# A gated attention and gelu MLP on one Trainium2 core: the gelu's square taken from ScalarE to GpSimd, and the copies of the turned maxima from ScalarE to VectorE

## The chip, the core and the metric

The kernel runs on one NeuronCore of one Trainium2 chip. The metric is the device time of one execution in microseconds (us). The kernel before takes 812.53 us, the median of three runs (812.45, 812.53 and 814.32). In the profile the engines have short names: PE is TensorE (its weight loads stand apart as PEld), DVE is VectorE, ACT is ScalarE, POOL is GpSimd, and SP is SyncE, which only issues transfers here.

## What is computed

```python
x = A_x                                    # 1 x 2048 x 512, float32
g = sigmoid((x * gate_w).sum(-1, keepdims=True))
# a: attention, 32 heads of 16, a query sees itself and the 255 keys before it
scores = q k^T * 16 ** -0.5, masked outside the window
a = (softmax(scores) v) @ wo               # wqkv is 512 x 1536, wo 512 x 512
# b: dense layers with a gelu (tanh form)
b = gelu(x @ w1 + b1) @ w2 + b2            # w1 is 512 x 1792, w2 1792 x 512
out = g * a + (1 - g) * b
```

## The kernel before

The dense products keep float32 accuracy by splitting each factor into a rounded high part and a low rest. The helper `mm3` (lines 100 to 103) then issues three matmuls, high by high, high by low and low by high. That is why each dense group in the profile appears three times, at L101, L102 and L103.

The program has three stretches. First come q, k and v for four blocks of 512 rows, until about 150 us. Then the attention and the MLP run interleaved until about 770 us. The output projection and the mix with the gate come last.

The attention goes in 128 units: 8 groups of 4 heads by 16 blocks of 128 keys. For each of a unit's 4 heads TensorE first computes scores `sm` with queries on the partitions (L389). VectorE adds the mask and takes each query's maximum in one custom instruction (L394; its output `jm` is scrap, the maximum goes to `M` by a short read of the accumulator). This runs six units ahead of the rest. Every two units the eight maxima per query are negated and laid out in `nm` by two small VectorE instructions (L405, L406). A matmul with the identity turns them so that queries lie along the free dimension (L413, PSUM tile `mp`). Two copies, one for each unit, put 16 rows of 256 numbers into rows 96 to 111 of `qs`, scaled by a column of `odd` that is 0 or 1 for each row (L418). The later score matmul `st` (L433) has these rows among its inputs and so subtracts the maximum. ScalarE takes the exponential into `pt` (L445), GpSimd zeroes what lies outside the window (L437, L440), and the products with v accumulate in `pv` (L465).

The MLP goes in eight passes, each over one half of the 1792 hidden columns and one block of 512 rows. A pass first makes 7 hidden tiles `u` (12 matmuls each), and then 4 output tiles `y` (21 matmuls each). I call these the u-phase and the y-phase of a pass. In the u-phase each tile goes through the gelu:

- `x1` = u + b1, ScalarE (L556)
- `sq` = (u + b1) squared, ScalarE, from PSUM (L559)
- `sq` = (sq + 22.36) * x1, VectorE (L562)
- `sq` = tanh of that, ScalarE (L565)
- `x1` = (sq + 1) * x1, VectorE (L568), then the high part `h[:, 0]`, VectorE (L571), then the low part `h[:, 1]`, GpSimd (L574)

Some buffers are scarce: `x1` and `sq` have two each, the PSUM tag `sm` (shared by `sm` and `mp`) three, `st` two, and `d` (for `u` and `y`) two.

The order on every engine is fixed while the program is built. A clock of planned nanoseconds moves with the matmuls that are written (`tick`), and `after(ns, fn)` writes a step into its engine's queue when that clock has passed. So a step's delay is only a place in the queue. On the chip an engine runs its queue strictly in order, and a step whose inputs are late holds everything behind it. The six delays of the gelu's steps after `x1` stand in the tuple `GELU`. Weights for later passes are loaded and split between the gelus: the high part on ScalarE (L156), the low part on GpSimd (L160).

Of the kernel before, what the change touches and what calls it, by code (L numbers as in the profile page):

```python
# [12 lines left out]
AF = mybir.ActivationFunctionType  # L13
ALU = mybir.AluOpType
# [18 lines left out]
def gated_mix(ctx: ExitStack, tc: tile.TileContext, x, wqkv, wo, w1, b1, w2, b2, gate_w, out):  # L33
    nc = tc.nc
# [10 lines left out]
    def f32(ap):  # L45
        return ap.bitcast(F32)
# [23 lines left out]
    b1c = cp.tile([128, NF], F32, name="b1c")  # L70
# [15 lines left out]
    odd = cp.tile([128, 2], F32, name="odd")  # L86
# [21 lines left out]
    def after(ns, fn, *args):  # L108
        now[1] += 1
        heapq.heappush(todo, (now[0] + ns, now[1], fn, args))  # L110
# [7 lines left out]
    def tick(ns):  # L118
        now[0] += ns
        while todo and todo[0][0] <= now[0]:  # L120
            step_todo()

    def need(*keys):
        for key in keys:
            while key not in done:
                step_todo()
# [51 lines left out]
    qs = cp.tile([128, 2, S], F32R, name="qs")  # L178
# [230 lines left out]
    def att_turn(g_, rb):  # L409

        need(("nm", g_, rb))
        p = ps.tile([112, 128], F32, tag="sm", bufs=3, name=f"mp{g_}_{rb}")
        nc.tensor.matmul(p, nms[rb % 2], identr, start=True, stop=True)  # L413

        def put():
            for b in range(RB):
                cols = slice((rb * RB + b) * 128, (rb * RB + b + 1) * 128)
                nc.scalar.activation(qs[96:112, :, cols], p[96:112].unsqueeze(1).broadcast_to([16, 2, 128]),  # L418
                    AF.Copy, scale=odd[96:112, b:b + 1])
            done.add(("rows", g_, rb))  # L420
        tick(67)
        after(100, put)
# [129 lines left out]
    def gelu(p, f, h):  # L552

        x1 = sb.tile([128, T], F32, tag="x1", bufs=2, name=f"x1{h.name}")
        sq = sb.tile([128, T], F32, tag="sq", bufs=2, name=f"sq{h.name}")
        nc.scalar.activation(x1, p, AF.Identity, bias=b1c[:, f:f + 1])  # L556

        def f1():
            nc.scalar.activation(sq, p, AF.Square, bias=b1c[:, f:f + 1])  # L559

        def f2():
            nc.vector.scalar_tensor_tensor(sq, sq, GC, x1, op0=ALU.add, op1=ALU.mult)  # L562

        def f3():
            nc.scalar.activation(sq, sq, AF.Tanh, scale=GS)  # L565

        def f4():
            nc.vector.scalar_tensor_tensor(x1, sq, 1.0, x1, op0=ALU.add, op1=ALU.mult)  # L568

        def f5():  # L570
            nc.vector.tensor_copy(h[:, 0], x1)  # L571

        def f6():
            nc.gpsimd.tensor_sub(h[:, 1], x1, f32(h[:, 0]))  # L574
            done.add(h.name)
        for ns, fn in zip(GELU, (f1, f2, f3, f4, f5, f6)):
            after(ns, fn)
# [168 lines left out]
LEAD = 6  # L746
START = 117e3
NORM = 6000
GELU = (700, 1500, 2300, 3300, 4200, 5000)
XAT = 3  # L750
ORDER = 'mspf'
XOR = 1
# [26 lines left out]
```

## Time and profile before

| profiled execution before | |
|---|---|
| its own time | 813.36 us |
| span in the trace | 811.4 us |
| PE busy | 788.5 us, 97% |
| DVE busy | 513.7 us, 63% |
| ACT busy | 483.4 us, 60% |
| POOL busy | 338.7 us, 42% |

The span runs from the first to the last instruction in the trace; the time of the execution holds 2.0 us more around it. A busy time is the union of an engine's instructions. In a table by windows each engine has its busy time and, in brackets, how many instructions; after them stand the clock that TensorE was granted, the DMA engines' share and GB/s. In a list of groups a row gives line, engine, operation, output and input, shape and count, then total busy us and mean ns of one, and then how long the engine sat idle just before such instructions and who ended that. A row of waits reads: who waited, for whom, us in total, how often, the longest.

### The profile page before, as it was taken

To read this page: it belongs to the slowest core of one execution; us is meant where nothing else is said; L and a number is where in the kernel's file an instruction comes from. 1 tells how busy PE (TensorE), PEld (TensorE's weight loads), DVE (VectorE), ACT (ScalarE), POOL (GpSimd) and SP (SyncE) were. 2 spreads that over 40 slices of the span, in tenths; PEclk is the share of its full clock that TensorE was granted. 3 is DMA by queue.
4 is the path that set the end of the run, shared out by engine and by line. 5 is a ranking of instruction groups with operands and counts; after the bars stand their busy time and mean duration, and the time that the engine had idled before them with its cause. 6 is when DMAs were issued, how large, how long until landed. Compare 5 with 4: busy or idle time off the path is not lost.

```text
span 811.4 us, 14841 instructions
## 1 busy us (share of the span) xinstructions
PE 788.5 (97%) x4694; PEld 616.6 (76%) x4694; DVE 513.7 (63%) x1517; ACT 483.4 (60%) x993; POOL 338.7 (42%) x611
## 2 busy tenths in 40 slices
PE   8999999999999999999999999999999999999998
PEld 6788888867877777688767867877777778777767
DVE  5433332887478758856885688568757865784353
ACT  4434423587568557755875677567656764876631
POOL 3200002396336425542784386336524552574100
PEclk9999999999999999999999999999999999999999
DMA  8985856536542734443234555542664363335873
GB/s 260 387 308 195 304 174 211 195 89 215 164 137 66 227 116 119 122 156 104 86 101 132 171 156 173 152 143 86 192 179 129 99 202 113 97 118 186 249 260 117
DMA packets 94925, 135.72 MB, mean 167 GB/s; under 512 B 32256, under 2 KB 43776, under 8 KB 94848
## 3 DMA queue, kind: packets, MB, share of 16 engines
q1 hardware_dynamic: 94848, 134.79, 52.3%
q8 instruction: 37, 0.61, 0.3%
q14 instruction: 40, 0.33, 0.1%
HBM read 79.70 MB, written 55.05 MB: 166 GB/s over the span
## 4 chain that ended last, share of the span: by engine, by line
PE 78%; DVE 8%; ACT 7%; DMA 2%; issue 2%; SPq 1%; POOL 1%; POOLq 0%; DVEq 0%; ACTq 0%
PE st L433 9%; PE pv L465 9%; PE sm L389 8%; PE y L101 6%; PE y L103 6%; PE y L102 6%; PE u L101 4%; PE u L102 4%; PE u L103 4%; PE qk L101 3%; PE qk L103 3%; PE qk L102 3%; DVE jm L394 2%; ACT pt L445 2%; PE v L103 2%
## 5 line engine op out<-in xcount | busy, mean ns | idle before, releaser
L394 DVE CUSTOM_DVE_ANT_0 jm<-sm,mask 128x384 bf16<-128x384 f32 (+2 forms) x512 | 270.6, 528 | 150.1 <-PE sm L389 128.7
L445 ACT ACTIVATE pt<-st 128x384 f32<-128x384 f32 (+2 forms) x512 | 231.0, 471 | 120.6 <-PE st L433 102.9
L437 POOL TENSOR_SCALAR_AFFINE_SELECT pt<-pt 128x256 f32<-128x256 f32 x256 | 122.3, 478 | 248.8 <-ACT pt L445 248.2
L433 PE MATMUL st<-qs,ks 128*128 128x384 f32 (+2 forms) x512 | 172.1, 338 | 8.1 <-ACT pt L445 7.1
L389 PE MATMUL sm<-ks,qs 96*128 96x384 f32 (+2 forms) x512 | 169.6, 332 | 1.8 <-DVE M L394 0.8
L433 PEld LDWEIGHTS st<-qs,ks 128*128 128x128 f32 x512 | 97.0, 190 | 37.1 <-ACT pt L445 19.4
L389 PEld LDWEIGHTS sm<-ks,qs 96*128 96x128 f32 x512 | 96.2, 188 | 26.0 <-DVE M L394 5.2
L440 POOL TENSOR_SCALAR_AFFINE_SELECT pt<-pt 128x256 f32<-128x256 f32 x224 | 101.9, 455 | 0.0
L465 PE MATMUL pv<-pt,vbuf 128*32 128x384 f32 (+2 forms) x1408 | 91.6, 389 | 0.1
L101 PE MATMUL y<-w,h 128*128 128x512 f32 x224 | 89.4, 399 | 0.0
L103 PE MATMUL y<-w,h 128*128 128x512 f32 x224 | 87.7, 391 | 1.3 <-POOL h L574 1.3
L102 PE MATMUL y<-w,h 128*128 128x512 f32 x224 | 87.7, 391 | 0.0
L574 POOL TENSOR_TENSOR h<-x1h,h 128x512 fp32r<-128x512 f32 x56 | 72.5, 1294 | 35.6 <-DVE h L571 35.2
L101 PE MATMUL u<-mx,w 128*128 128x512 f32 x196 | 79.3, 404 | 0.0
L102 PE MATMUL u<-mx,w 128*128 128x512 f32 x196 | 76.7, 391 | 0.0
L103 PE MATMUL u<-mx,w 128*128 128x512 f32 x196 | 76.6, 391 | 0.0
L418 ACT ACTIVATE qs<-mp,odd 16x256 fp32r<-16x256 f32 x128 | 53.0, 460 | 38.9 <-PE mp L413 37.9
L465 PEld LDWEIGHTS pv<-pt,vbuf 128*32 128x32 f32 x1408 | 38.5, 109 | 37.2 <-issue 24.2
L562 DVE SCALAR_TENSOR_TENSOR sqh<-sqh,x1h 128x512 f32<-128x512 f32 x56 | 51.6, 921 | 13.2 <-ACT sqh L559 13.2
L565 ACT ACTIVATE sqh<-sqh 128x512 f32<-128x512 f32 x56 | 35.5, 634 | 36.8 <-DVE sqh L562 36.2
L160 POOL TENSOR_TENSOR w<-raw_w,w 128x512 fp32r<-128x512 f32 x28 | 38.4, 1370 | 40.3 <-ACT w L156 40.2
L256 DVE TENSOR_TENSOR qke<-qk,qke 128x512 fp32r<-128x512 f32 x32 | 22.1, 691 | 51.3 <-ACT qke L253 49.6
(122 smaller groups left out, 1247.7 us busy)
## 6 DMA issues: line engine op xcount, KB each, us to landing
mx<-XT SPq DMA_DIRECT2D x24, 512.0 KB
SQ<-qke SPq DMA_DIRECT2D x16, 512.0 KB
SK<-qke SPq DMA_DIRECT2D x16, 512.0 KB
qs<-SQ SPq DMA_DIRECT2D x64, 128.0 KB
ND<-nd SPq DMA_DIRECT2D x32, 256.0 KB
ks<-SK SPq DMA_DIRECT2D x60, 128.0 KB
raw_w<-in_B_w_dram SPq DMA_DIRECT2D x28, 256.0 KB
SV<-vx SPq DMA_DIRECT2D x16, 272.0 KB
```

The costliest lines, as they stand in the source:

```text
L101: nc.tensor.matmul(p, lh, rh, start=first, stop=False)
L102: nc.tensor.matmul(p, lh, rl, start=False, stop=False)
L103: nc.tensor.matmul(p, ll, rh, start=False, stop=last)
L389: nc.tensor.matmul(p[:, :w], qs[0:96, pr, b * 128:(b + 1) * 128], ks[0:96, pr, s, k0:k0 + w], start=True, stop=True)
L394: nc.vector.tensor_tensor_reduce(junk[:, :w], p[:, :w], mask[:, 384 - w:384], 1.0, -3e38, ALU.add, ALU.max, M[:, b % RB, i:i + 1])
L418: nc.scalar.activation(qs[96:112, :, cols], p[96:112].unsqueeze(1).broadcast_to([16, 2, 128]), AF.Copy, scale=odd[96:112, b:b + 1])
L433: nc.tensor.matmul(p[:, :w], ks[:, pr, s, kb * 128:(kb + 1) * 128], qs[:, pr, kb * 128:kb * 128 + w], start=True, stop=True)
L437: nc.gpsimd.affine_select(out=pt[:, :, 0:128], in_=pt[:, :, 0:128], pattern=[[0, 2], [1, 128]], compare_op=ALU.is_ge, fill=0.0, base=0, ch ...
L440: nc.gpsimd.affine_select(out=pt[:, :, 256:384], in_=pt[:, :, 256:384], pattern=[[0, 2], [-1, 128]], compare_op=ALU.is_ge, fill=0.0, base= ...
L445: nc.scalar.activation(pt[:, s, :w], p[:, :w], AF.Exp, scale=SCALE)
L465: nc.tensor.matmul(pv[32 * i:32 * i + 32, q - c * T:e - c * T], vt[:, 68 * (kb % NB) + 17 * i:68 * (kb % NB) + 17 * i + 32], pts[g_, kb, i ...
L574: nc.gpsimd.tensor_sub(h[:, 1], x1, f32(h[:, 0]))
```

## The change

Two steps leave ScalarE, and the planned delays of the gelu change with them. The copies of the turned maxima become a `tensor_scalar` on VectorE, with the same input (PSUM, each row read twice), the same scale and the same place in the program. The square becomes a product of `x1` with itself on GpSimd; it reads `x1` from SBUF, since GpSimd is given no PSUM tile in this kernel. The first delay stays 700, the others grow by 700.

```diff
@@ att_turn
         def put():
             for b in range(RB):
                 cols = slice((rb * RB + b) * 128, (rb * RB + b + 1) * 128)
-                nc.scalar.activation(qs[96:112, :, cols], p[96:112].unsqueeze(1).broadcast_to([16, 2, 128]),
-                    AF.Copy, scale=odd[96:112, b:b + 1])
+                nc.vector.tensor_scalar(qs[96:112, :, cols], p[96:112].unsqueeze(1).broadcast_to([16, 2, 128]),
+                                        odd[96:112, b:b + 1], None, op0=ALU.mult)
@@ gelu
         def f1():
-            nc.scalar.activation(sq, p, AF.Square, bias=b1c[:, f:f + 1])
+            nc.gpsimd.tensor_mul(sq, x1, x1)
@@
-GELU = (700, 1500, 2300, 3300, 4200, 5000)
+GELU = (700, 2200, 3000, 4000, 4900, 5700)
```

TensorE's queue is the same in both kernels, instruction by instruction. On VectorE, here is a piece of the third u-phase in the kernel before. In a name like `sqh1_3` the numbers are the block of rows and the hidden tile; `jm2_10_3` is group 2, unit 10, head 3; longer numbers only count buffers.

```order
L406 SCALAR_TENSOR_TENSOR nm0_170<-M2_8_3688,nm0_170 128x8
L394 ISA jm2_10_0_3843,M2_10_3820<-sm2_10_0_3841,mask_140 128x384
L394 ISA M2_10_3820 128x1
L562 SCALAR_TENSOR_TENSOR sqh1_4_3829_3836<-sqh1_4_3829_3836,x1h1_4_3829_3835 128x512
L394 ISA jm2_10_3_3857,M2_10_3820<-sm2_10_3_3855,mask_140 128x384
L394 ISA M2_10_3820 128x1
L568 SCALAR_TENSOR_TENSOR x1h1_4_3829_3835<-sqh1_4_3829_3836,x1h1_4_3829_3835 128x512
L394 ISA jm2_10_2_3885,M2_10_3820<-sm2_10_2_3883,mask_140 128x384
```

And this is the same piece of VectorE's queue in the changed kernel.

```order
L406 SCALAR_TENSOR_TENSOR nm0_170<-M2_8_3687,nm0_170 128x8
L394 ISA jm2_10_0_3842,M2_10_3820<-sm2_10_0_3840,mask_140 128x384
L394 ISA M2_10_3820 128x1
L394 ISA jm2_10_3_3856,M2_10_3820<-sm2_10_3_3854,mask_140 128x384
L394 ISA M2_10_3820 128x1
L562 SCALAR_TENSOR_TENSOR sqh1_4_3828_3835<-sqh1_4_3828_3835,x1h1_4_3828_3834 128x512
L418 TENSOR_SCALAR qs_179<-mp2_4_3872,odd_164 16x2x128 x2
L394 ISA jm2_10_2_3884,M2_10_3820<-sm2_10_2_3882,mask_140 128x384
L568 SCALAR_TENSOR_TENSOR x1h1_4_3828_3834<-sqh1_4_3828_3835,x1h1_4_3828_3834 128x512
```

The gelu's first VectorE step stands one maximum later than before, and the two copies of the turned maxima stand between it and the next maximum.

On GpSimd, this is the same place before: the selects (L437, L440) of units 3 and 4, and the low part of tile 3.

```order
L437 AFFINE_SELECT pt2_3_0_3774<-pt2_3_0_3774 128x2x128
L440 AFFINE_SELECT pt2_3_0_3774<-pt2_3_0_3774 128x2x128
L437 AFFINE_SELECT pt2_3_1_3798<-pt2_3_1_3798 128x2x128
L440 AFFINE_SELECT pt2_3_1_3798<-pt2_3_1_3798 128x2x128
L574 TENSOR_TENSOR h1_3_3758<-x1h1_3_3758_3764,h1_3_3758 128x512
L437 AFFINE_SELECT pt2_4_0_3824<-pt2_4_0_3824 128x2x128
```

And in the changed kernel:

```order
L559 TENSOR_TENSOR sqh1_3_3757_3765<-x1h1_3_3757_3764 128x512
L437 AFFINE_SELECT pt2_3_0_3774<-pt2_3_0_3774 128x2x128
L440 AFFINE_SELECT pt2_3_0_3774<-pt2_3_0_3774 128x2x128
L437 AFFINE_SELECT pt2_3_1_3797<-pt2_3_1_3797 128x2x128
L440 AFFINE_SELECT pt2_3_1_3797<-pt2_3_1_3797 128x2x128
L559 TENSOR_TENSOR sqh1_4_3828_3835<-x1h1_4_3828_3834 128x512
L574 TENSOR_TENSOR h1_3_3757<-x1h1_3_3757_3764,h1_3_3757 128x512
L437 AFFINE_SELECT pt2_4_0_3824<-pt2_4_0_3824 128x2x128
```

A square now stands behind the selects of the unit before it, and the low part of the tile before stands right beside it.

## The prediction

> **What bounds the kernel now.** I read the head of the page first.
>
> ```profile
> span 811.4 us, 14841 instructions
> PE 788.5 (97%) x4694; PEld 616.6 (76%) x4694; DVE 513.7 (63%) x1517; ACT 483.4 (60%) x993; POOL 338.7 (42%) x611
> PE 78%; DVE 8%; ACT 7%; DMA 2%; issue 2%; SPq 1%; POOL 1%; POOLq 0%; DVEq 0%; ACTq 0%
> ```
>
> TensorE is busy all but 22.9 us, and its queue doesn't change, so nothing can be won beyond that. But VectorE and ScalarE hold 15% of the chain that ended last, so there are places where they set the pace. The table by windows, one for each u-phase, shows where (first, fifth and last of eight, and their sum).
>
> ```profile
> 161.00:197.00 36.00, 33.74 (x197) 25.06 (x196) 31.18 (x85) 27.86 (x58) 30.86 (x42) 1.00 0.46 139
> ...
> 467.60:508.50 40.90, 38.41 (x230) 28.30 (x230) 35.55 (x94) 30.93 (x66) 30.95 (x44) 1.00 0.53 167
> ...
> 698.00:737.60 39.60, 37.83 (x233) 29.04 (x233) 33.72 (x94) 30.75 (x65) 30.17 (x45) 1.00 0.35 105
> sum 307.80, PE 294.82 PEld 222.47 DVE 261.58 ACT 234.59 POOL 217.43; mean PE 36.85 PEld 27.81 DVE 32.70 ACT 29.32 POOL 27.18
> ```
>
> The same for the seven y-phases with a u-phase behind them:
>
> ```profile
> 197.00:234.50 37.50, 37.50 (x255) 29.98 (x254) 21.32 (x82) 20.79 (x47) 11.64 (x30) 1.00 0.56 173
> ...
> sum 262.20, PE 262.19 PEld 208.29 DVE 153.88 ACT 148.43 POOL 83.80; mean PE 37.46 PEld 29.76 DVE 21.98 ACT 21.20 POOL 11.97
> ```
>
> In the y-phases TensorE never pauses and VectorE is busy 59%: what is added to it there is hidden. In the u-phases TensorE loses 307.8 - 294.8 = 13.0 us. That is the prize, if ScalarE is what holds it up. VectorE is busy 85% there, ScalarE 76%, GpSimd 71%. What each waits for there says who leads. First the waits over the whole run, then VectorE's wait for scores in the first and the last u-phase.
>
> ```profile
> ACT sqh L565 <- DVE sqh L562: 36.2, 34, 2.5
> PEld st L433 <- ACT pt L445: 19.4, 39, 1.4
> DVE sqh L562 <- ACT sqh L559: 13.2, 21, 1.1
> DVE x1h L568 <- ACT sqh L565: 7.5, 15, 0.8
> PE st L433 <- ACT pt L445: 7.1, 15, 1.1
> ```
>
> ```profile
> DVE jm L394 <- PE sm L389: 0.9, 2, 0.5
> ```
>
> ```profile
> DVE jm L394 <- PE sm L389: 1.7, 2, 1.4
> ```
>
> TensorE's pauses name ScalarE's exponentials, which suggests that ScalarE is at fault. But ScalarE's own longest wait in the gelu is 36.2 us for VectorE's step L562, and the exponentials stand behind that wait. VectorE's waits for scores in the eight windows are 0.9, 2.8, 2.1, 1.4, 0.3, 3.2, 1.3 and 1.7 us, 13.7 in all. With 13.2 and 7.5 for ScalarE it waits 34.4 us; busy and waits make 296.0 of 307.8, and the other 11.8 are gaps between its instructions. So VectorE is occupied for 273 of 308 us, and only 13.7 us of it is room that TensorE leaves. VectorE is the engine nearest its limit where the time is lost, and the change gives it more.
>
> **The change part by part.** The rows that carry the prices, from the groups:
>
> ```profile
> L418 ACT ACTIVATE qs<-mp,odd 16x256 fp32r<-16x256 f32 x128 | 53.0, 460 | 38.9 <-PE mp L413 37.9
> L559 ACT ACTIVATE sqh<-u,b1c 128x512 f32<-128x512 f32 x56 | 38.5, 687 | 0.0
> ```
>
> ```profile
> L437 POOL TENSOR_SCALAR_AFFINE_SELECT pt<-pt 128x256 f32<-128x256 f32 x256 | 122.3, 478 | 248.8 <-ACT pt L445 248.2
> L440 POOL TENSOR_SCALAR_AFFINE_SELECT pt<-pt 128x256 f32<-128x256 f32 x224 | 101.9, 455 | 0.0
> L160 POOL TENSOR_TENSOR w<-raw_w,w 128x512 fp32r<-128x512 f32 x28 | 38.4, 1370 | 40.3 <-ACT w L156 40.2
> L413 PE MATMUL mp<-identr,nm 128*112 128x128 f32 x64 | 19.8, 310 | 2.2 <-DVE nm L406 2.1
> L574 POOL TENSOR_TENSOR h<-x1h,h 128x512 fp32r<-128x512 f32 x56 | 72.5, 1294 | 35.6 <-DVE h L571 35.2 <-DVE nm L405 0.4
> L394 DVE CUSTOM_DVE_ANT_0 jm<-sm,mask 128x384 bf16<-128x384 f32 x448 | 247.7, 553 | 99.9 <-PE sm L389 79.4 <-PE st L433 1.0
> L394 DVE CUSTOM_DVE_ANT_0 jm<-sm,mask 128x256 bf16<-128x256 f32 x32 | 13.6, 424 | 13.2 <-PE sm L389 12.6
> L394 DVE CUSTOM_DVE_ANT_0 jm<-sm,mask 128x128 bf16<-128x128 f32 x32 | 9.3, 290 | 37.1 <-PE sm L389 36.7
> L668 DVE SCALAR_TENSOR_TENSOR ao<-a,g,yb 128x256 f32<-128x256 f32 x2 | 1.0, 484 | 1.6 <-PE a L103 1.6
> L562 DVE SCALAR_TENSOR_TENSOR sqh<-sqh,x1h 128x512 f32<-128x512 f32 x56 | 51.6, 921 | 13.2 <-ACT sqh L559 13.2
> L405 DVE TENSOR_SCALAR nm<-M 128x8 fp32r<-128x8 f32 x64 | 22.4, 350 | 0.0
> L406 DVE SCALAR_TENSOR_TENSOR nm<-M,nm 128x8 fp32r<-128x8 f32 x64 | 17.7, 277 | 2.2
> ```
>
> ```profile
> L418 ACT ACTIVATE qs<-mp,odd x128: 450/461/472, 143.5 to 741.4; 16x256 fp32r<-16x256 f32 x128
> ```
>
> ScalarE loses 53.0 + 38.5 = 91.5 us of 483.4. In the u-phases that is all of the square, and 308/598 of the copies (the L418 instructions run evenly from 143.5 to 741.4 us, two every two units): 38.5 + 27 = 66 of 235 us. It drops to 55% there.
>
> *The copies on VectorE.* No row shows this instruction. Its nearest kin reads 256 numbers a partition from PSUM and takes 424 ns; from below there is 290 ns for 128 numbers, from above 484 ns for 256 with two more operands. I take 424. There are 128 in 64 pairs, and about 33 pairs fall into u-phases: 33 x 2 x 0.42 = 28 us, less a little overlap of each pair, 26 us. Ends: 33 x 2 x 0.29 = 19, and 33 x 2 x 0.484 = 32. [...]
>
> The copies wait for the turning matmul, and maxima and gelu steps stand behind them in VectorE's queue. The next scores come behind that matmul on TensorE anyway, so I charge nothing for the wait; without that cover it is up to the matmul's 0.31 us a pair, 10 us.
>
> *The square on GpSimd.* The nearest row is L574, 1294 ns: 56 x 1.29 = 72 us, against 38.5 on ScalarE. A single operand read twice might make it cheaper, but 512 numbers in a select of twice 256 already take 0.48 + 0.46 = 0.94 us by the rows of L437 and L440, so 0.9 us would be the low end. GpSimd then has 217 + 72 = 290 of 308 us in the u-phases.
>
> *What that does to VectorE.* Two places of the trace show the engines stopping each other.
>
> ```profile
> 177.23 1.29 POOL L160 TENSOR_TENSOR w<-raw_w,w 128x512 fp32r<-128x512 f32 x1
> ```
>
> ```profile
> 177.29 1.77 DVE L562 SCALAR_TENSOR_TENSOR sqh<-sqh,x1h 128x512 f32<-128x512 f32 x1 [0.38 <-ACT sqh L559]
> ```
>
> ```profile
> 328.78 1.29 POOL L574 TENSOR_TENSOR h<-x1h,h 128x512 fp32r<-128x512 f32 x1
> 328.94 0.08 DVE L394 DVE_READ_ACCUMULATOR2_ANT M<- 128x1 f32 x1
> 328.94 1.16 DVE L405 TENSOR_SCALAR nm<-M 128x8 fp32r<-128x8 f32 x1
> ```
>
> An L405 of 8 numbers takes 1.16 us, until GpSimd's instruction is over; alone it takes 158 ns, and L562 677, L406 167.
>
> ```profile
> L405 DVE TENSOR_SCALAR nm<-M x64: 158/210/1157, 142.2 to 738.0; 128x8 fp32r<-128x8 f32 x64
> ```
>
> ```profile
> L562 DVE SCALAR_TENSOR_TENSOR sqh<-sqh,x1h x56: 677/775/1775, 155.1 to 730.6; 128x512 f32<-128x512 f32 x56
> ```
>
> ```profile
> L406 DVE SCALAR_TENSOR_TENSOR nm<-M,nm x64: 167/171/1279, 142.4 to 738.2; 128x8 fp32r<-128x8 f32 x64
> ```
>
> Means less shortest times give 56 x 0.244 + 64 x 0.192 + 64 x 0.110 = 33 us lost today. Spread over GpSimd's 338.7 us that is 0.10 for each, so 72 us more cost 7; put down to the 56 + 28 long two-input instructions alone (L574, L160), it is 0.39 each, so 56 more cost 22. I take the middle, 14. [...]
>
> *Waits inside the gelu.* The square used to follow `x1` at once; now it ends 1.29 - 0.69 = 0.6 us later, plus GpSimd's queue. L562 stands one maximum later in VectorE's queue (553 ns and the read behind it). These cancel, so I leave the 13.2 us. ScalarE is freer, so of the 7.5 us for the tanh I take off half, 4. GpSimd's queue I charge with 4 us, for the four u-phases (first, fourth, fifth, last) in which weights are split too: the first would have 30.9 + 9.0 = 39.9 us of GpSimd in 36.
>
> *The sum.* On VectorE in the u-phases: 26 + 14 + 4 - 4 = 40 us more, of which 13.7 go into the room that TensorE leaves: +26. Some of each phase's delay can be carried into its y-phase, but the three `sm` buffers let TensorE run only about two maxima ahead, by the 424 ns row under 1 us a phase, and the phases end with such a lag today already; I take off 2. So +24 us on the execution's 813.4: 837.4. The profiled execution lies 0.8 us above the median, so against the median 836.5.
>
> **The rivals.**
>
> *ScalarE was the brake* (faster). For it: TensorE's waits of 7.1 and 19.4 us name the exponentials, and 66 us leave that engine. Then most of the 13.0 us come back: 10 off, 813.4 - 10 - 0.8 = 802.6 us. It decides if VectorE's added work stays under its 13.7 us of room, say copies at 0.2 us and no stopping. Against: ScalarE's 36.2 us of waiting for VectorE, and the 290 ns that even 128 numbers take.
>
> *All hidden* (no change). If the copies cost 19 and the stops 7, and all 20.7 us in which VectorE waits for ScalarE vanish, VectorE has 5 us more to do, well inside its 13.7: 812.5 us. Against: the square only changes the engine on which VectorE waits for it.
>
> *GpSimd becomes the bound* (slower still). It would be 290 of 308 us occupied, in order, with each square behind selects that wait for exponentials, while VectorE's maxima stand behind L562 that waits for the square. If each square comes 0.5 us later than the next maximum can cover, 56 x 0.5 = 28 us are added to the +24, and I count 20 of them, since VectorE's other delays hide the rest: 813.4 + 44 - 0.8 = 856.6. For it: 290 of 308 us leave hardly room for an engine that must keep its order. Against: L437's 248.2 us of waiting for exponentials get shorter when ScalarE is freer.
>
> That the moves don't take place is excluded by the order of the changed program.
>
> **How the numbers follow.** Chances: the forecast 0.68, GpSimd as bound 0.17, ScalarE as brake 0.10, all hidden 0.05. The low end takes the cheap ends, 19 + 7 and no queue, less 13.7 and all 7.5: +5, so 817.4 against the median. The high end takes the GpSimd rival's 856.6 and half of the dear copies' 6 us more: 860. Left out are the two cases on the other side, 0.15, and a few hundredths above. A difference under 0.3%, 2.4 us, can't be told from none here. Faster 0.10, same 0.05, slower 0.85.
>
> **What would show it.** Right: the u-phases' windows grow from 38.5 (307.8 over 8) to about 41.5 us while the y-phases stay at 37.5; VectorE waits for scores under 0.7 us a u-phase; L418 near 424 ns; L562, L405 and L406 gain in mean; TensorE's waits name maxima (L394) and L418. Wrong: u-phases no longer than before, or VectorE waiting more for TensorE than today; L562 waiting mostly for the square of L559 on GpSimd would speak for the GpSimd rival.

## The result, and the profile after

The changed kernel takes 856.67 us, the median of six runs (853.16 to 857.95), against 812.96 us for the kernel before in six runs (812.45 to 814.83). That is slower by a ratio of 1.0528, with a 95% interval of 1.0506 to 1.0551, or 42.9 us by the ratio (41.1 to 44.8). The profiled execution took 856.19 us. The forecast of 836.5 us had the sign and the place; its size is a good half of what came, and the time lies near the upper end of its range (817.4 to 860). This is the head of the page of the changed kernel, with the shares of the chain that ended last.

```profile
span 854.5 us, 14799 instructions
PE 801.9 (94%) x4694; PEld 623.1 (73%) x4694; DVE 593.7 (69%) x1645; ACT 398.4 (47%) x809; POOL 403.5 (47%) x667
PE 68%; DVE 15%; POOL 7%; issue 6%; ACT 3%; DMA 1%; SPq 0%; POOLq 0%; DVEq 0%; ACTq 0%
```

ScalarE lost 85.0 us (483.4 to 398.4; the prediction's two rows add up to 91.5, but a busy time counts instructions that overlap once) and the kernel became slower. VectorE's and GpSimd's part of the chain rose from 9% to 22%.

First the place. TensorE runs the same 4694 matmuls in the same order in both traces, so a stretch of the program can be cut at the same score matmuls in each. The prediction's windows for the "u-phases" start some 11 us after a pass's first `u` matmul and reach as far into the `y` matmuls: they are really the stretches in which the gelus run. I call them gelu stretches and cut all kernels there. These are the first and the last of the changed kernel and the sum of all eight.

```profile
161.60:204.20 42.60, 35.33 (x196) 26.08 (x195) 38.28 (x88) 22.50 (x47) 34.95 (x46) 0.96 0.31 101
...
734.80:780.70 45.90, 40.53 (x233) 29.62 (x232) 39.09 (x102) 24.49 (x51) 37.71 (x51) 0.96 0.30 92
sum 347.70, PE 302.75 PEld 225.01 DVE 307.85 ACT 181.10 POOL 271.82; mean PE 37.84 PEld 28.13 DVE 38.48 ACT 22.64 POOL 33.98
```

The kernel before, cut at the same matmuls (a hair other than in the prediction):

```profile
sum 305.60, PE 292.57 PEld 221.16 DVE 259.19 ACT 232.22 POOL 215.33; mean PE 36.57 PEld 27.65 DVE 32.40 ACT 29.03 POOL 26.92
```

The gelu stretches grew by 42.1 us, which is all but about 1 us of the span's 43.1. TensorE pauses in them for 347.7 - 302.8 = 44.9 us instead of 13.0. The seven quiet stretches between them have 271.4 us against 270.2, TensorE busy throughout. VectorE is busy 89% of the gelu stretches, GpSimd 78%, ScalarE only 52%.

Next, what TensorE waits for. The changed kernel (who waited, for whom, us, times, longest), then the kernel before:

```profile
PE st L433 <- ACT pt L445: 19.1, 16, 2.4
PE sm L389 <- DVE qs L418: 9.7, 13, 1.1
PE mp L413 <- DVE nm L406: 9.3, 9, 2.6
PE sm L389 <- DVE M L394: 4.4, 10, 0.6
```

```profile
PE mp L413 <- DVE nm L406: 2.1, 2, 1.3
PE sm L389 <- DVE M L394: 0.8, 3, 0.4
PE sm L389 <- ACT qs L418: 0.8, 2, 0.5
```

With the 7.1 us for exponentials that the prediction shows, TensorE's waits grew by 12.0 for the exponentials, 8.9 for the copies, 7.2 for the laid-out maxima and 3.6 for the maxima: 31.7 us of the 42. The other 10 us are matmuls that took longer: TensorE is busy 302.8 us in the stretches instead of 292.6 (last section). ScalarE and VectorE in the gelu, changed kernel:

```profile
ACT sqh L565 <- DVE sqh L562: 111.3, 55, 6.0
DVE sqh L562 <- POOL sqh L559: 12.5, 23, 1.4
```

The tanh (L565) waits 111.3 us for L562, three times the 36.2 of before, and the exponentials stand behind it in ScalarE's queue. So ScalarE, with 18% less to do, delivers later. The groups of the instructions that the prediction priced:

```profile
L562 DVE SCALAR_TENSOR_TENSOR sqh<-sqh,x1h 128x512 f32<-128x512 f32 x56 | 58.8, 1049 | 12.8 <-POOL sqh L559 12.5
L418 DVE TENSOR_SCALAR qs<-mp,odd 16x256 fp32r<-16x256 f32 x128 | 57.7, 488 | 35.3 <-PE mp L413 34.2
L559 POOL TENSOR_TENSOR sqh<-x1h 128x512 f32<-128x512 f32 x56 | 60.2, 1075 | 8.4 <-ACT x1h L556 8.1
L406 DVE SCALAR_TENSOR_TENSOR nm<-M,nm 128x8 fp32r<-128x8 f32 x64 | 28.3, 442 | 2.2
L405 DVE TENSOR_SCALAR nm<-M 128x8 fp32r<-128x8 f32 x64 | 18.3, 286 | 0.0
```

VectorE's busy time rose by 80.0 us. The copies are 57.7 of that; the other 22.3 lie on instructions that were there before, L406 (277 to 442 ns), L562 (921 to 1049) and L571 (486 to 585) above all, while L405 became shorter (350 to 286). One place from the timeline of the changed kernel shows how an instruction is held (start, length, instruction):

```profile
341.71 1.20 POOL L559 TENSOR_TENSOR sqh<-x1h 128x512 f32<-128x512 f32 x1
341.93 1.00 DVE L405 TENSOR_SCALAR nm<-M 128x8 fp32r<-128x8 f32 x1
342.87 1.26 POOL L574 TENSOR_TENSOR h<-x1h,h 128x512 fp32r<-128x512 f32 x1
342.97 1.18 DVE L406 SCALAR_TENSOR_TENSOR nm<-M,nm 128x8 fp32r<-128x8 f32 x1
344.21 0.32 PE L413 MATMUL mp<-identr,nm 128*112 128x128 f32 x1 [1.54 <-DVE nm L406]
345.25 0.69 DVE L562 SCALAR_TENSOR_TENSOR sqh<-sqh,x1h 128x512 f32<-128x512 f32 x1
345.97 0.63 ACT L565 ACTIVATE sqh<-sqh 128x512 f32<-128x512 f32 x1 [2.64 <-DVE sqh L562]
```

The square starts first. L405, of eight numbers, ends only when the square has ended: 1.00 us for what takes 0.158 alone. The low part L574 stands right behind the square, as the new order puts it, and L406 ends with it, after 1.18 us. TensorE meanwhile has waited 1.54 us for L406, and the tanh waits 2.64 us for L562, which stands behind all this on VectorE.

### The profile page after: what moved, and what is told of

Same layout as the page of the kernel before. It is cut to its first block, busy times and chain, and to the rows that moved or that the text cites. A ratio compares the mean times of both kernels' runs of the same rounds, so it can differ in the third digit from the quotient of the medians.

```text
span 854.5 us, 14799 instructions
## 1 busy us (share of the span) xinstructions
PE 801.9 (94%) x4694; PEld 623.1 (73%) x4694; DVE 593.7 (69%) x1645; ACT 398.4 (47%) x809; POOL 403.5 (47%) x667
## 4 chain that ended last, share of the span: by engine, by line
PE 68%; DVE 15%; POOL 7%; issue 6%; ACT 3%; DMA 1%; SPq 0%; POOLq 0%; DVEq 0%; ACTq 0%
PE st L433 7%; PE sm L389 7%; PE pv L465 7%; PE y L101 5%; PE y L103 5%; PE y L102 5%; DVE jm L394 4%; DVE sqh L562 4%; PE qk L101 4%; PE qk L103 3%; PE qk L102 3%; PE u L101 3%; PE u L102 3%; PE u L103 3%; POOL sqh L559 2%
## 5 line engine op out<-in xcount | busy, mean ns | idle before, releaser
L437 POOL TENSOR_SCALAR_AFFINE_SELECT pt<-pt 128x256 f32<-128x256 f32 x256 | 123.7, 483 | 231.0 <-ACT pt L445 226.8
L433 PE MATMUL st<-qs,ks 128*128 128x384 f32 (+2 forms) x512 | 172.3, 338 | 19.9 <-ACT pt L445 19.1
L389 PE MATMUL sm<-ks,qs 96*128 96x384 f32 (+2 forms) x512 | 172.2, 337 | 14.5 <-DVE qs L418 9.7
L389 PEld LDWEIGHTS sm<-ks,qs 96*128 96x128 f32 x512 | 97.2, 190 | 44.9 <-DVE M L394 9.8
L440 POOL TENSOR_SCALAR_AFFINE_SELECT pt<-pt 128x256 f32<-128x256 f32 x224 | 109.4, 488 | 0.0
L465 PE MATMUL pv<-pt,vbuf 128*32 128x384 f32 (+2 forms) x1408 | 93.6, 393 | 0.1
L565 ACT ACTIVATE sqh<-sqh 128x512 f32<-128x512 f32 x56 | 35.3, 631 | 111.3 <-DVE sqh L562 111.3
L574 POOL TENSOR_TENSOR h<-x1h,h 128x512 fp32r<-128x512 f32 x56 | 72.2, 1290 | 26.8 <-DVE h L571 26.0
L418 DVE TENSOR_SCALAR qs<-mp,odd 16x256 fp32r<-16x256 f32 x128 | 57.7, 488 | 35.3 <-PE mp L413 34.2
L101 PE MATMUL u<-mx,w 128*128 128x512 f32 x196 | 80.6, 411 | 0.0
L102 PE MATMUL u<-mx,w 128*128 128x512 f32 x196 | 77.7, 397 | 0.0
L103 PE MATMUL u<-mx,w 128*128 128x512 f32 x196 | 77.5, 395 | 0.0
L562 DVE SCALAR_TENSOR_TENSOR sqh<-sqh,x1h 128x512 f32<-128x512 f32 x56 | 58.8, 1049 | 12.8 <-POOL sqh L559 12.5
L465 PEld LDWEIGHTS pv<-pt,vbuf 128*32 128x32 f32 x1408 | 39.0, 110 | 38.5 <-issue 25.4
L559 POOL TENSOR_TENSOR sqh<-x1h 128x512 f32<-128x512 f32 x56 | 60.2, 1075 | 8.4 <-ACT x1h L556 8.1
```

What stands on the lines that cost most here:

```text
L101: nc.tensor.matmul(p, lh, rh, start=first, stop=False)
L102: nc.tensor.matmul(p, lh, rl, start=False, stop=False)
L103: nc.tensor.matmul(p, ll, rh, start=False, stop=last)
L389: nc.tensor.matmul(p[:, :w], qs[0:96, pr, b * 128:(b + 1) * 128], ks[0:96, pr, s, k0:k0 + w], start=True, stop=True)
L433: nc.tensor.matmul(p[:, :w], ks[:, pr, s, kb * 128:(kb + 1) * 128], qs[:, pr, kb * 128:kb * 128 + w], start=True, stop=True)
L437: nc.gpsimd.affine_select(out=pt[:, :, 0:128], in_=pt[:, :, 0:128], pattern=[[0, 2], [1, 128]], compare_op=ALU.is_ge, fill=0.0, base=0, ch ...
```

## The experiments

Three theories stood. *VectorE's time*: the change puts more on VectorE in the gelu stretches, and that alone is the loss. *The square on GpSimd*: the loss comes from where the square is computed, by its stops of VectorE, by its lateness in the in-order queues, or by both. *Queue places*: the new delays (`GELU`) put the gelu's later steps further back. Each kernel is compared with the kernel before in the same session, whose median was 813.53 us in the first, 813.21 in the second and 812.64 in the third set.

### One part at a time

**Copies alone.** Only the copies of the turned maxima go to VectorE; square and delays stay.

```diff
-                nc.scalar.activation(qs[96:112, :, cols], p[96:112].unsqueeze(1).broadcast_to([16, 2, 128]),
-                    AF.Copy, scale=odd[96:112, b:b + 1])
+                nc.vector.tensor_scalar(qs[96:112, :, cols], p[96:112].unsqueeze(1).broadcast_to([16, 2, 128]),
+                                        odd[96:112, b:b + 1], None, op0=ALU.mult)
```

> Only the copies of the turned maxima move to VectorE; square and delays as before. If VectorE's occupancy is the cause: a pair of copies measured 0.416 + 0.488 = 0.90 us, 33 pairs in u-phases are 30 us, less the 13.7 us of room: 10 to 18 us slower than before, 823 to 831. If GpSimd's square is the cause of the 44 us: within 3 us of before, 810 to 816.

Measured: 819.77 us, ratio 1.0071 (1.0048 to 1.0094), 5.8 us more. That is under what VectorE's time alone asked for, and above nothing. The sum over its gelu stretches:

```profile
sum 312.80, PE 293.96 PEld 221.78 DVE 285.48 ACT 206.32 POOL 215.60; mean PE 36.74 PEld 27.72 DVE 35.69 ACT 25.79 POOL 26.95
```

VectorE has 26.3 us more there, as forecast, and the stretches grow by only 7.2. Summed over the eight stretches, its waits for scores fall from 13.3 to 2.7 us and its waits for ScalarE in L562 and L568 from 17.3 to 4.0: 23.9 us of the 26.3 are taken out of waiting.

**Square alone.** The square goes to GpSimd with the new delays; the copies stay on ScalarE.

```diff
-            nc.scalar.activation(sq, p, AF.Square, bias=b1c[:, f:f + 1])
+            nc.gpsimd.tensor_mul(sq, x1, x1)
...
-GELU = (700, 1500, 2300, 3300, 4200, 5000)
+GELU = (700, 2200, 3000, 4000, 4900, 5700)
```

> Only the square moves to GpSimd, with the new delays; the copies stay on ScalarE. If VectorE's occupancy is the cause: 20 us of stops less 13.7 us of room and a few us of clock: 5 to 14 us slower, 818 to 827. If GpSimd's square and its place in the chain are the cause: 30 us slower or more, 843 to 857.

Measured: 856.38 us, ratio 1.0522 (1.0483 to 1.0561): the whole loss, without the copies. The theory of VectorE's time alone falls here, since the copies' 26 us are missing from VectorE and nothing is gained by it. Its waits:

```profile
ACT sqh L565 <- DVE sqh L562: 100.7, 54, 4.0
DVE sqh L562 <- POOL sqh L559: 31.4, 33, 2.3
PE st L433 <- ACT pt L445: 27.0, 22, 2.4
```

**Both, with the old delays.** The changed kernel with `GELU` as it was.

> Both moves with the delays of before. If VectorE's occupancy is the cause, its work is the same and only the wait for the square grows, which was 12.5 us: 853 to 866. If GpSimd's place in the chain is the cause, the first VectorE step of the gelu stands 0.7 us too early, 56 x 0.7 = 39 us: 870 to 896.

Measured: 877.05 us, ratio 1.0772 (1.0743 to 1.0801), 20 us worse than the changed kernel. Its waits on TensorE:

```profile
PE sm L389 <- DVE M L394: 22.1, 30, 2.5
PE sm L389 <- DVE qs L418: 17.3, 15, 2.8
PE mp L413 <- DVE nm L406: 7.3, 12, 1.7
PE st L433 <- ACT pt L445: 6.6, 8, 2.1
```

L562 now stands so early that VectorE waits 40.0 us in it for the square, and what stands behind it, maxima and copies, comes late; the exponentials don't. The later places trade one wait for the other.

**Delays alone.** The kernel before with the changed kernel's `GELU`.

> The kernel before with the new delays alone; no instruction changes its engine. Both theories expect little: if the delays carry nothing, 810 to 816. Should they be a cause of their own (steps of the gelu later in VectorE's queue, the next tile's x1 held up), 3 to 10 us slower.

Measured: 816.62 us, ratio 1.0038 (1.0026 to 1.0050). With the square still on ScalarE the later places cost 3 us; TensorE's waits for exponentials grow from 7.1 to 13.7 us.

### What the square costs by merely running on GpSimd

**Idle square.** The kernel before, and with each square on ScalarE a product of the same size on GpSimd that reads a constant and that nobody reads. It is work added to the computation.

```diff
             nc.scalar.activation(sq, p, AF.Square, bias=b1c[:, f:f + 1])
+            junk = sb.tile([128, T], BF16, tag="pj", bufs=1, name=f"pj{h.name}")
+            nc.gpsimd.tensor_mul(junk, b2b, b2b)
```

> The kernel before, everything on ScalarE as it was, plus one product of a constant 128x512 tile with itself on GpSimd for each gelu, into scrap that nobody reads. Nobody waits for it, so only its occupation of GpSimd and its stops of VectorE remain. If the stops are the cost: 835 to 857. If the wait for the square is the cost: 812 to 822.

Measured: 832.25 us, ratio 1.0239 (1.0210 to 1.0267): 19.4 us from an instruction on which nothing depends. It lies between the two expectations, so it is a part of the loss and not all of it. Its groups, and two of TensorE's waits:

```profile
L406 DVE SCALAR_TENSOR_TENSOR nm<-M,nm 128x8 fp32r<-128x8 f32 x64 | 25.5, 399 | 2.2
L405 DVE TENSOR_SCALAR nm<-M 128x8 fp32r<-128x8 f32 x64 | 25.4, 396 | 0.0
PE mp L413 <- DVE nm L406: 4.6, 9, 0.9
PE pv L465 <- POOL pt L437: 3.2, 1, 3.2
```

And the sum over its gelu stretches:

```profile
sum 321.90, PE 301.63 PEld 223.19 DVE 275.98 ACT 232.12 POOL 275.00; mean PE 37.70 PEld 27.90 DVE 34.50 ACT 29.02 POOL 34.37
```

VectorE is busy 16.8 us more in the stretches, and they grow by 16.3. Its waits for scores there are 13.3 us, as before to the tenth. This added work doesn't use the room that the copies used. But not all of it need be stops of VectorE: TensorE's products with v (L465) wait 4.6 us for selects on GpSimd (3.2 us in the row above and 1.4 for L440), for which they don't wait in the kernel before, and only 2.5 us more for L406. The extra product makes GpSimd's own queue late too. In the changed kernel TensorE has no such wait.

**Idle memset.** The same with an instruction that only writes, of a similar length (948 ns against 1171).

```diff
+            junk = sb.tile([128, 1024], BF16, tag="pj", bufs=1, name=f"pj{h.name}")
+            nc.gpsimd.memset(junk, 0.0)
```

> The kernel before plus a memset of 128x1024 bf16 (about 1 us) on GpSimd for each gelu, into scrap. It holds GpSimd's queue about as long as the square, but reads nothing. If GpSimd's occupied queue is the cost: as slow as with the idle square. If stops through reads are the cost: 812 to 820. Should a write stop VectorE as well: between the two.

Measured: 827.68 us, ratio 1.0180 (1.0156 to 1.0204), 14.6 us: between 820 and the idle square. Its groups:

```profile
L405 DVE TENSOR_SCALAR nm<-M 128x8 fp32r<-128x8 f32 x64 | 32.2, 503 | 0.0
L564 DVE SCALAR_TENSOR_TENSOR sqh<-sqh,x1h 128x512 f32<-128x512 f32 x56 | 48.0, 857 | 10.7 <-ACT sqh L559 10.6
```

L405 is stopped more than ever (350 ns before, 503), while L562 (L564 in this kernel) is not (921 before, 857); L406, which also has two inputs, rose a little (277 to 311). In the timeline from 175 us on, ten L405 take over 1 us, up to 2.05, and nine of them end within 0.04 us of a memset's end. Nine L564 take over 1 us there, and each ends 0.54 to 0.56 us after a low part (L576) or a weight split (L160), none after a memset. Why L405 and L564 differ the runs don't show. VectorE's busy time rose by 13.2 us over the whole run with the memset and by 19.3 with the product, against 14.6 and 19.4 us of time: close to one for one in both. That doesn't show that stops alone are the cost. By the length of the two instructions on GpSimd the memset would cost 19.4 x 948 / 1171 = 15.7 us, an estimate just as near, and TensorE waits 3.1 us for selects here as well. The two runs don't separate stops of VectorE from GpSimd's occupied queue.

**The square in four pieces.** The changed kernel with the product cut into four of 128 columns: if a stop lasts until the GpSimd instruction ends, it would end after a quarter.

```diff
-            nc.gpsimd.tensor_mul(sq, x1, x1)
+            for k in range(4):
+                nc.gpsimd.tensor_mul(sq[:, k * 128:(k + 1) * 128], x1[:, k * 128:(k + 1) * 128], x1[:, k * 128:(k + 1) * 128])
```

> The changed kernel with the square on GpSimd as four products of 128 columns each instead of one of 512. If the cost is that a long GpSimd instruction stops VectorE's two-input steps for its whole length (0.7 to 0.9 us a hit), a stop ends after a quarter: 825 to 845. If the cost is that VectorE waits for the square at the end of GpSimd's queue, four pieces take longer than one: 857 to 875.

Measured: 873.0 us, ratio 1.0739 (1.0692 to 1.0785), slower still by 16 us.

```profile
L560 POOL TENSOR_TENSOR sqh<-x1h 128x128 f32<-128x128 f32 x224 | 85.6, 412 | 8.4 <-ACT x1h L556 8.2
L563 DVE SCALAR_TENSOR_TENSOR sqh<-sqh,x1h 128x512 f32<-128x512 f32 x56 | 70.9, 1265 | 29.2 <-POOL sqh L560 28.9
```

The small steps were freed (L405 225 ns, L406 294), but L562 (L563 here) was held longer, 1265 ns against 1049, so that VectorE's busy time stayed as it was (593.3 us against 593.7): the stops moved and didn't shrink. Four pieces make 4 x 412 = 1.65 us of square, and VectorE waits 28.9 us for it instead of 12.5. With the same VectorE work the kernel lost 16 us, so when the square is ready counts too.

### What the square costs as a link of the chain

**Copies and an idle square.** Copies on VectorE, the square in use still on ScalarE, the idle product on GpSimd, old delays. VectorE and GpSimd then carry what they carry in the changed kernel, but nobody waits for GpSimd's square.

> Copies on VectorE, the square still on ScalarE for use, and an idle product on GpSimd that nobody waits for. If copies and stops add up on VectorE's time, with no part for the square as an input, it comes near the changed kernel: 847 to 858. If each has only its own effect (5.7 and 19 us), so that some 20 us of the changed kernel belong to the square as a link of the chain: 833 to 843.

Measured: 838.83 us, ratio 1.0313 (1.0286 to 1.0339), 25.4 us: the copies' 5.8 and the idle square's 19.4, added up. Its page and waits (L564 and L567 are L562 and L565):

```profile
PE 798.4 (96%) x4694; PEld 617.9 (74%) x4694; DVE 592.4 (71%) x1645; ACT 427.8 (51%) x865; POOL 406.9 (49%) x667
```

```profile
ACT sqh L567 <- DVE sqh L564: 69.6, 49, 3.6
PE sm L389 <- DVE qs L418: 11.7, 11, 2.6
PE mp L413 <- DVE nm L406: 4.7, 10, 0.9
PE st L433 <- ACT pt L445: 2.3, 7, 0.5
```

VectorE has 592.4 us here and 593.7 in the changed kernel: the same work to 1.3 us, and 17.8 us between the two times. What differs most on TensorE is its wait for exponentials, 2.3 us here and 19.1 there. So some 18 us of the change belong to the square as a link between ScalarE's `x1` and VectorE's L562, with the delays that this needs.

**Later places.** The square alone, and the whole change, with the steps after the square another 1000 planned ns back.

```diff
-GELU = (700, 2200, 3000, 4000, 4900, 5700)
+GELU = (700, 3200, 4000, 5000, 5900, 6700)
```

> Only the square on GpSimd, copies on ScalarE, and every later step of the gelu 1000 planned ns later still: (700, 3200, 4000, 5000, 5900, 6700). VectorE waited 31.4 us for the square with the square alone, 13.2 before. If that wait is what the square costs beyond its stops of VectorE, it falls under 15 us and the time to 835 to 846. If later steps only move the loss on (tanh and exponentials behind them, x1 held longer): 850 to 865.

> The changed kernel with the same later delays. Its wait for the square was 12.5 us. If VectorE's time is the cause, at most those 12 us can come back: 845 to 856. If the longer chain through the gelu is the cause, later steps make it longer: 858 to 875.

Measured: 845.53 us, ratio 1.0401 (1.0364 to 1.0438), for the square alone, and 846.64, ratio 1.0407 (1.0369 to 1.0444), for both. Each gets about 10 us back. The whole change in these places:

```profile
PE st L433 <- ACT pt L445: 13.7, 15, 1.9
DVE sqh L562 <- POOL sqh L559: 1.4, 3, 0.6
```

VectorE's wait for the square is gone (12.5 to 1.4), and with it 10 of the 18 us. About 8 us remain above the copies with the idle square, and so does most of the wait for exponentials (13.7 of 19.1 us), while the tanh still waits 90.1 us for L562. That the gelu's chain, now as long as the square makes it, ends later would account for it; no run tests that by itself. No version with either move beat the kernel before.

### Two more tries on who holds whom

**The cast on ScalarE.** The kernel before, with the high part of the hidden tile (L571) moved from VectorE to ScalarE. If VectorE's time were the bound, this would win.

```diff
-            nc.vector.tensor_copy(h[:, 0], x1)
+            nc.scalar.activation(h[:, 0], x1, AF.Copy)
```

> The kernel before with the gelu's copy of the high part on ScalarE (56 x 0.63 us) instead of VectorE (56 x 0.49 us). If VectorE's work in the u-phases sets the pace: 804 to 811. If what ScalarE does is as tight (235 + 35 of 308 us): 814 to 830.

Measured: 830.61 us, ratio 1.0209 (1.0184 to 1.0233). VectorE's busy time fell by 27.5 us, to 486.2, and the kernel lost 17. Its waits:

```profile
DVE sqh L562 <- ACT sqh L559: 32.8, 41, 2.5
ACT h L571 <- DVE x1h L568: 23.1, 27, 2.1
PE st L433 <- ACT pt L445: 18.4, 34, 1.1
```

One more hand-over between two in-order queues, and both wait for each other. Busy time taken from the busier engine was paid back in waits.

**One copy of each pair.** The first copy on VectorE, the second on ScalarE.

```diff
+                if b == 0:
+                    nc.vector.tensor_scalar(qs[96:112, :, cols], p[96:112].unsqueeze(1).broadcast_to([16, 2, 128]),
+                                            odd[96:112, b:b + 1], None, op0=ALU.mult)
+                else:
+                    nc.scalar.activation(qs[96:112, :, cols], p[96:112].unsqueeze(1).broadcast_to([16, 2, 128]),
+                                         AF.Copy, scale=odd[96:112, b:b + 1])
```

> The kernel before with one copy of each pair on VectorE and the other on ScalarE. VectorE's added 15 us in the u-phases are about its room of 13.7, ScalarE loses 13: if the room is really there, 809 to 815. If VectorE has no room: 816 to 822.

Measured: 829.19 us, ratio 1.0193 (1.0162 to 1.0224), outside both expectations, and no clean test. Both copies write the same `qs`, and the one on ScalarE (L422 here) waited for the one on VectorE:

```profile
ACT qs L422 <- DVE qs L419: 81.3, 46, 3.9
```

The pair has become a chain, and the run says nothing of half the copies' price.

## Why the prediction was right or wrong

**The sum.** By the ratios the 42.9 us are about 6 for the copies (copies alone), 19 for the square's running on GpSimd (idle square: stops of VectorE and a later GpSimd queue together) and 18 for the square as a link (what remains over copies with an idle square). In the same three groups the forecast had 26 - 4 - 13.7 - 2 = 6 for the copies, 14 for the stops and 4 for GpSimd's queue, 24 in all. These parts hold in this order of adding: on top of the square in use the copies cost nothing that can be told (856.38 without them, 856.67 with them).

**What bounds: right in place, half right in reading.** The loss lies in the gelu stretches, the quiet ones don't move, and ScalarE is not the brake. But "VectorE is the engine nearest its limit" was too simple a bound. With the cast taken off it the kernel got slower, and with the same VectorE work it runs in 838.8 or in 856.7 us. The working also put the whole run's 13.2 and 7.5 us of waits for ScalarE into the u-phases; 11.2 and 6.1 lie in the gelu stretches. Of its signs, the copies' time and VectorE's few waits for scores (2.6 us in the stretches) came, but L405's mean fell (350 to 286 ns) and TensorE's longest wait names the exponentials, not the maxima.

**The copies: the size right, by an exchange of terms.** An instruction takes 488 ns, not 424, and a pair 0.90 us, where the forecast's 26 us over 33 pairs make 0.79; but in the run with the copies alone only 31 pairs fall into the gelu stretches, not 33. So VectorE's time there rose by 26.3 us, the forecast's 26, by luck in part. They use up 10.6 of the 13.3 us of waits for scores, as forecast. The waits for ScalarE fell by 13.3 instead of 4, since L562's wait for the square on ScalarE went with them. That new wait of the copies for the turning matmul, which was charged with nothing, is 1.2 us in the changed kernel's gelu stretches; the row's other 33 us fall elsewhere.

**The square's running on GpSimd: mis-sized, and with a cover that it doesn't have.** 14 us of stops was the middle of 7 and 22, and VectorE's old instructions gained 22.3 us: the dear end. The forecast netted all of VectorE's delays against one sum of room. The idle square cost 19.4 us and left that room unused (13.3 us of waits for scores, as before). Where a stop strikes can explain that: in the piece of timeline above it is at L405 and L406, just before the matmul that TensorE has next. How much of the 19.4 us is stops, and how much is selects that come later from GpSimd, the runs don't show.

**The step that failed** is that of the waits inside the gelu: "These cancel, so I leave the 13.2 us", with 4 us for GpSimd's queue. That price was about 18. L562's wait kept its total (13.2, now 12.5), so the row alone looks like the forecast. But it changed its cause. With the copies on VectorE, a square on ScalarE leaves only 0.8 us of it in the gelu stretches (copies with an idle square), so all 12.4 of the changed kernel there are the square on GpSimd. And the tanh's wait of 111.3 us with the exponentials behind it was in no term.

**The rivals.** ScalarE as brake would have given 802.6: it fell to 52% busy in the gelu stretches and the loss is there. All hidden is out too. *GpSimd becomes the bound* gave 856.6, which is the time that came. Its sign was that L562 waits for L559 on GpSimd, and it does. That the number fits is luck, since its working, 28 us of waits in VectorE of which 20 count, isn't what the runs show: about 12 us of such waits lie in the gelu stretches, about 10 us come back when they are removed, the other 8 are open (below), and GpSimd is not full: it is busy 78% of the gelu stretches, and the changed order with later places runs 10 us faster with the same GpSimd work.

**What stays open.** The 19.4 us of the idle square aren't split between stops of VectorE and GpSimd's later selects. The 8 us that remain with later places aren't split between the later steps and TensorE's clock. In the idle square only about 7 us of the 18 on the span show as pauses of TensorE (829.3 - 799.5 = 29.8 against 22.9 us), 4.6 of them for selects; the other 11 are longer matmuls, of which the clock can explain up to 5. A cheaper place for the square on GpSimd, away from L405 and L406, was not tried.

## What to carry to other kernels

Before work is moved off an engine, look at who waits in that engine's queue and for whom: ScalarE waited for VectorE inside the gelu (36.2 us for L562), so freeing ScalarE of 85.0 us freed nothing, and with a third engine in the chain that wait became 111.3 us. The square, 1075 ns on GpSimd with SBUF operands, had a second price in this kernel: it held small VectorE steps (an L405 took 1.00 us instead of 0.158) and delayed what stood behind it on GpSimd (with the idle square TensorE waits 4.6 us for selects). A product that nobody reads cost 19.4 us, although VectorE kept its 13.3 us of idle time before the scores. To price such a move, add the moved instruction first as work that nobody reads; the difference to the real move is the price of the dependence, with the new order that it needs.

## What the runs showed of the hardware that was not expected

In the profiled execution of the changed kernel TensorE's granted clock fell to half five times before the end, for 3.4 us each, and in that of the kernel before not until the end. Here is one such window and the 3.4 us ahead of it (TensorE's busy time is the first entry, the clock the third from the end):

```profile
494.90:498.30 3.40, 0.95 (x12) 0.13 (x4) 2.68 (x3) 0.89 (x2) 3.34 (x4) 1.00 0.57 139
498.30:501.70 3.40, 3.23 (x9) 2.75 (x10) 3.40 (x8) 0.00 (x0) 1.38 (x2) 0.50 0.74 210
```

And another:

```profile
174.00:177.40 3.40, 1.75 (x8) 1.31 (x9) 3.34 (x7) 1.39 (x3) 3.35 (x4) 1.00 0.11 24
177.40:180.80 3.40, 3.40 (x10) 2.82 (x10) 2.73 (x9) 1.81 (x4) 3.02 (x5) 0.51 0.38 98
```

In the second, consecutive `u` matmuls start 0.43 us apart; after it, from 181.04 us on, 0.23. The five starts lie on one grid: 79, 94, 100 and 167 times 3.413 us after the first. Cut on that grid, the windows ahead of the five are the least busy of all from 140 to 790 us: TensorE was busy in them for 0.96 to 1.80 of 3.41 us, 28% to 53%. The next, with 1.81 us, was not followed by half clock; since the ends of matmuls are modelled, this trace shows no exact limit. Its poorest windows were thus paid for a second time: five windows at half speed cost up to 5 x 1.7 = 8.5 us, part of the matmuls' longer time. The windows at half clock add up to 17.1 us in the changed kernel (mean clock 0.989), 3.4 with the copies alone (0.998), 10.2 with the idle square (0.994), 3.4 with copies and idle square (0.998), 20.5 with the square alone (0.988) and 27.3 with the old delays (0.984). TensorE was never idle for a whole such window: its longest pause ahead of the five was 2.6 us.

The square was cheaper than the low part of the same shape, 1075 ns against the 1294 that the prediction took from L574; it reads one tile twice where L574 reads two, and writes f32 where L574 writes fp32r, and neither was tested by itself. The idle product, also of one operand with itself but with a bf16 output, took 1171 ns.
